# Moving two ScalarE operations of a weight conversion to its first step, and a subtraction behind the readers of a closed accumulator

## The chip, the cores and the metric

The kernel runs on one core of one Trainium2 chip. The metric is the device time of one execution in microseconds (us). The core's engines run side by side, each through its own list of instructions in order, and wait for each other by semaphores. PE is TensorE (matrix products, with PEld its weight loads), DVE is VectorE, ACT is ScalarE, POOL is GpSimd, SP only issues transfers.

## What is computed

An attention block with a position bias feeds a gated layer, and that feeds a second gated layer with a normalisation. Cut to what matters here:

```python
x = attention(q, k, v, bias)                  # 1152 tokens x 512
gate = 1.0 / (1.0 + np.exp(-(x @ w_gate)))    # 512 x 1536
val = x @ w_val
x = (gate * val) @ w_out                      # 1536 x 512
xn = x / rms(x) * rms_g                       # second layer
g = xn @ w_gate2
out = (g * sigmoid(g) * (xn @ w_val2)) @ w_out2
```

All matrix products of the two gated layers are made from split operands: a value is a high part that the fast product form holds exactly, and a low part that is the rest. Each product is three matmuls: high by high, high by low, low by high.

## The kernel before

**Weights.** They arrive as 64-bit numbers and are converted on the chip. One piece is 128 x 512 weights, loaded as pairs of 32-bit words (`wr`: the low word `lw`, the high word `hw`, so each word stands 8 bytes from the next of its kind). There are 72 pieces. `piece_step(k, i)` is one of four steps ("micro steps") on piece k. Step 0: DVE shifts the high word (`tt`, L471). Step 1: ACT takes the absolute value (`ab`, L480), DVE joins the sign (`ff`, L482), ACT scales the low word (`rb`, L484), and POOL adds it (`ff`, L485). Step 2: DVE multiplies (`ab`, L489), and ACT writes the high part into a ring of 24 slots (`wh` or `wv`, L490). Step 3: DVE subtracts to get the low part (`wl` or `wv`, L494).

**Order of the micro steps.** `advance(limit, micro)` issues micro steps: it goes round the four kinds in a fixed order and issues one whose `ready` is true. `tt` and `rb` have one buffer each, `ff` two, `ab` and `wr` three. `fetch` issues a load when the piece two before has passed step 1.

**The gated layers.** `STEPS` lists 72 steps s: a layer, a group g of 2 to 4 blocks of 128 hidden rows, a chunk c of 384 tokens, and a block f of the group. `gate_val(s)` issues 24 matmuls on PE (`gv`, L509), then `sg` on ACT (L513), `g` on DVE (L515), `gh` on ACT (L517). `low_part(s)` is one DVE subtraction (`gl`, L523). `out_mm(s)` is 12 matmuls (L539) into an accumulator `acc` of four PSUM parts, two pairs of banks. On PE the order is gv(s), out(s-2), gv(s+1), out(s-1) and so on. When a group's blocks for a chunk are all in, the accumulator is closed, and `collect` adds its four parts to `part` in SBUF: by four DVE additions (L547), and in the first group by two ACT copies (L551) and two DVE copies (L549). The next chunk's accumulator takes the same banks, so the next `out_mm` on PE waits for these readers. `closing(s - 2)` is true in the loop's step s in which the collect is issued. Some micro steps, five in most steps, are issued around `low_part` and `out_mm`; in a closing step all five follow.

**Before the gated layers** come 40 units of attention, the last eighteen with one micro step each, and a passage of four in which attention ends: there gv(0) is issued, and ACT evicts transposed blocks (`pt`, L703) that PE's product `pv` (L399) waits for.

Of the kernel before, what the change touches and what calls it, by code (L numbers as in the profile page):

```python
# [8 lines left out]
F32 = mybir.dt.float32  # L9
F32R = mybir.dt.float32r  # L10
U32 = mybir.dt.uint32
I32 = mybir.dt.int32
AF = mybir.ActivationFunctionType
ALU = mybir.AluOpType
# [60 lines left out]
def fused_kernel(ctx: ExitStack, tc: tile.TileContext, qk, vp, tab, pcol, invp, prm, wts, rg, out):  # L75
    nc = tc.nc
# [351 lines left out]
    def members(l, g):  # L428
        a = sum(GROUPS[l][:g])
        return range(a, a + GROUPS[l][g])  # L430
# [7 lines left out]
    NS = len(STEPS)  # L438
# [5 lines left out]
    wraw = {}  # L444
    mid = {}
# [21 lines left out]
    def piece_step(k, i):  # L467
        mc = pools["mc"]
        if i == 0:
            tt = mc.tile([128, 512], U32, tag="tt", name=f"tt{k}")  # L470
            nc.vector.tensor_scalar(  # L471
                tt, wraw[k][:, :, 1], 3, 0x3FFFFFFF, op0=ALU.logical_shift_left, op1=ALU.bitwise_and
            )
            mid[k] = tt
        elif i == 1:
            raw = wraw.pop(k)
            lw, hw = raw[:, :, 0], raw[:, :, 1]
            tt = mid[k]
            ab = mc.tile([128, 512], F32, tag="ab", name=f"ab{k}", bufs=3)
            nc.scalar.activation(ab, hw.bitcast(F32), AF.Abs)  # L480
            ff = mc.tile([128, 512], U32, tag="ff", name=f"ff{k}", bufs=2)
            nc.vector.scalar_tensor_tensor(ff, hw, 0xC0000000, tt, op0=ALU.bitwise_and, op1=ALU.bitwise_or)  # L482
            rb = mc.tile([128, 512], I32, tag="rb", name=f"rb{k}")
            nc.scalar.activation(rb, lw, AF.Copy, scale=2.0**-29)  # L484
            nc.gpsimd.tensor_tensor(ff.bitcast(I32), ff.bitcast(I32), rb, op=ALU.add)  # L485
            mid[k] = (ab, ff)
        elif i == 2:
            ab, ff = mid[k]
            nc.vector.scalar_tensor_tensor(ab, ab, TINY_HI, ff.bitcast(F32), op0=ALU.is_ge, op1=ALU.mult)  # L489
            nc.scalar.activation(ring[k % RING][0], ab, AF.Copy)  # L490
        else:
            ab, _ = mid.pop(k)
            hi, lo = ring[k % RING]
            nc.vector.tensor_tensor(lo, ab, hi.bitcast(F32), op=ALU.subtract)  # L494
            wp[PIECES[k]] = (hi, lo)
# [24 lines left out]
    def low_part(s):  # L520
        gh, g32 = gt[s]
        gl = pools["me"].tile([128, CH], F32R, tag="gl", name=f"gl{s}", bufs=3)
        nc.vector.tensor_tensor(gl, g32, gh.bitcast(F32), op=ALU.subtract)  # L523
        gt[s] = (gh, gl)

    def out_mm(s):
        l, g, c, f = STEPS[s]
        gh, gl = gt.pop(s)
        oh, ol = wp[l, f, 2]
        head, last = f == members(l, g)[0], f == members(l, g)[-1]  # L530
        final = g == len(GROUPS[l]) - 1
        if head:
            acc[c] = (bank2(f"acc{l}{g}{c}a"), bank2(f"acc{l}{g}{c}b"))
        a = acc[c]
        cs = slice(c * CH, c * CH + CH)
        def product(m):
            dst = a[m % 2][:, m // 2, :CH]
            for k, (st_, mv) in enumerate(((oh, gh), (oh, gl), (ol, gh))):
                nc.tensor.matmul(  # L539
                    dst, st_[:, m * 128 : m * 128 + 128], mv, start=(head and k == 0), stop=(last and k == 2)  # L540
                )

        def collect(m):
            dst = a[m % 2][:, m // 2, :CH]
            pt = part[m][:, cs]
            if g > 0:
                nc.vector.tensor_tensor(pt, dst, pt, op=ALU.add)  # L547
            elif m % 2:
                nc.vector.tensor_copy(pt, dst)  # L549
            else:  # L550
                nc.scalar.activation(pt, dst, AF.Copy)  # L551
            if final and l == 1:
                (nc.sync if m % 2 == 0 else nc.scalar).dma_start(out[m * 128 : m * 128 + 128, cs], pt)


        for m in range(NCC):
            product(m)
            if s == NS - 1:
                collect(m)
        if not last:  # L560
            return
        if s < NS - 1:
            for m in range(NCC):
                collect(m)
        if final and l == 0:
            norm_queue.append([s + 2, c, 0, None])
# [52 lines left out]
    done = [0, 0, 0, 0]  # L619
    loaded = [0]  # L620
    phase = [0]
# [7 lines left out]
    def closing(s):  # L629
        return 0 <= s < NS - 1 and STEPS[s][:3] != STEPS[s + 1][:3]  # L630
# [9 lines left out]
    def ready(i):  # L640
        k = done[i]
        if k >= (NPC if i == 0 else done[i - 1]):
            return False
        if i == 0:
            return k < loaded[0] and done[1] >= k
        if i == 1:
            return done[2] >= k - 1 and done[3] >= k - 2
        return i == 3 or k < room[0]
# [10 lines left out]
    def advance(limit, micro):  # L659
        room[0] = limit  # L660
        idle = 0
        while micro and idle < 4:
            fetch()
            i = (2, 1, 0, 3)[phase[0]]
            phase[0] = (phase[0] + 1) % 4
            if ready(i):
                piece_step(done[i], i)
                done[i] += 1
                micro -= 1
                idle = 0  # L670
            else:
                idle += 1
# [79 lines left out]
    for s in range(EARLY + MORE, RING):  # L752
        tag, size = ("pt", 9 * 128) if s < EARLY + MORE + 2 else ("v", 1024)
# [5 lines left out]
    for s in range(NS + 2):  # L759
        while s < NS and (STEPS[s][0], STEPS[s][3], 1) not in wp:  # L760
            advance(done[3] + 1, 1)
        if 0 < s < NS:
            gate_val(s)
        micro = pace(s)
        if any(q[0] <= s for q in norm_queue):
            micro = min(micro, 2)

        parts = (0, micro) if closing(s - 2) else (micro // 2, micro - micro // 2)
        for half in range(2):
            k = done[3]  # L770
            if k < NPC:
                lim = k
                while lim < NPC and lim < k + 3 and (lim < RING or released(lim - RING) <= s):
                    lim += 1
                advance(lim, parts[half])
            if half == 0:
                if s < NS:
                    low_part(s)
                if s > 1:
                    l, _, _, f = STEPS[s - 2]  # L780
                    while (l, f, 2) not in wp:
                        advance(done[3] + 1, 1)
                    out_mm(s - 2)
                while norm_queue and norm_queue[0][0] <= s:
                    _, c, stage, box = norm_queue.pop(0)
                    norm_stage(c, stage, box)
                    if stage < 3:
                        norm_queue.append([s + 1, c, stage + 1, box])
# [68 lines left out]
```

## Time and profile before

| what | value |
|---|---|
| time of the kernel before, median of 3 runs | 667.5 us (665.89 to 667.67) |
| the profiled execution's own time | 664.12 us |
| its span | 662.3 us |
| PE busy | 643.4 us, 97% |
| DVE, ACT, POOL busy | 454.8, 348.6, 211.6 us |
| granted TensorE clock | 0.999 of full speed |

The span runs from the first to the last instruction; the 1.8 us between it and the execution's time lie around it. Attention takes the first 198 us, and the two gated layers fill the rest. Busy shares tell little here: what counts is where PE stands still.

### The profile page before, as it was taken

The numbers are of one execution on the slowest core, as the hardware profiler recorded it, in microseconds if no ns is written. First come the engines' busy times: TensorE is split into PE (matmuls) and PEld (weight loads), VectorE is DVE, ScalarE is ACT, GpSimd is POOL, SyncE is SP. The second block draws the span as 40 slices with busy tenths as digits, with TensorE's granted clock in tenths as the row PEclk, the third lists the DMA queues.
The fourth block names the chain that finished last, engine by engine and source line by source line (L and its number), as shares of the span: only waits on it lengthen the run. The fifth ranks groups of instructions, "written<-read, shape, count | busy, mean of one in ns | idle before, by whom it ended". The sixth has DMA issues, their size and how long they took to land.

```text
span 662.3 us, 11825 instructions
## 1 busy us (share of the span) xinstructions
PE 643.4 (97%) x4454; PEld 575.6 (87%) x4454; DVE 454.8 (69%) x968; ACT 348.6 (53%) x743; POOL 211.6 (32%) x259
## 2 busy tenths in 40 slices
PE   8889999999999899999999999999999999999997
PEld 4236666777679899999999999999999999999997
DVE  6997898688656667867677678788777777321322
ACT  4648889798685555444444564553555545211110
POOL 6566677476453322222222221110223223000000
PEclk9999999999999999999999999999999999999999
DMA  8866855663124333323233332111234330000111
GB/s 212 276 234 191 226 185 184 232 215 98 50 66 127 104 120 95 96 97 102 93 112 108 96 95 65 64 55 42 84 108 117 98 105 33 1 0 1 48 48 48
DMA packets 28088, 71.73 MB, mean 108 GB/s; under 512 B 3456, under 2 KB 6528, under 8 KB 28032
## 3 DMA queue, kind: packets, MB, share of 16 engines
q1 hardware_dynamic: 27168, 69.80, 34.2%
q10 hardware_dynamic: 864, 1.18, 0.5%
q8 instruction: 35, 0.57, 0.3%
q14 instruction: 21, 0.17, 0.1%
HBM read 57.72 MB, written 13.25 MB: 107 GB/s over the span
## 4 chain that ended last, share of the span: by engine, by line
PE 61%; DVE 13%; ACT 12%; issue 5%; POOL 5%; POOLq 0%; DVEq 0%
PE gv L509 26%; PE s L310 6%; PE pv L399 6%; PE tp L379 6%; POOL ff L485 4%; DVE ab L489 4%; ACT ab L480 3%; ACT rb L484 3%; PE bps L211 3%; DVE part L547 2%; DVE g L515 2%; ACT sg L513 2%; ACT gh L517 1%; ACT wh L490 1%; DVE tt L471 1%
## 5 line engine op out<-in xcount | busy, mean ns | idle before, releaser
L485 POOL TENSOR_TENSOR ff<-ff,rb 128x512 int32<-128x512 int32 x72 | 96.5, 1341 | 284.5 <-ACT rb L484 216.2
L515 DVE TENSOR_TENSOR g<-gv,sg 128x384 f32<-128x384 f32 x72 | 40.1, 558 | 112.5 <-PE gv L509 66.7
L517 ACT ACTIVATE gh<-g 128x384 fp32r<-128x384 f32 x72 | 37.9, 526 | 76.4 <-DVE g L515 76.4
L509 PE MATMUL gv<-nh,wv 128*128 128x384 f32 x288 | 76.5, 337 | 0.0
L509 PE MATMUL gv<-xh,wh 128*128 128x384 f32 x216 | 73.2, 339 | 0.0
L509 PE MATMUL gv<-xl,wh 128*128 128x384 f32 x216 | 72.9, 337 | 0.0
L509 PE MATMUL gv<-xh,wl 128*128 128x384 f32 x216 | 72.9, 337 | 0.0
L489 DVE SCALAR_TENSOR_TENSOR ab<-ab,ff 128x512 f32<-128x512 f32 x72 | 49.9, 693 | 28.7 <-POOL ff L485 28.7
L361 POOL TENSOR_SCALAR p<-p,rs 128x576 f32<-128x576 f32 x72 | 60.4, 847 | 13.4 <-DVE rs L359 13.1
L490 ACT ACTIVATE wh<-ab 128x512 fp32r<-128x512 f32 x42 | 26.5, 631 | 66.9 <-DVE ab L489 66.8
L328 DVE CUSTOM_DVE_ANT_0 t<-s,bt 128x576 f32<-128x576 f32 x72 | 51.8, 751 | 13.8 <-PE s L310 12.3
L193 DVE TENSOR_SCALAR ht<-w1l,bpc 128x304 f32<-128x304 f32 (+17 forms) x100 | 58.8, 652 | 0.0
L513 ACT ACTIVATE sg<-gv 128x384 f32<-128x384 f32 x72 | 34.5, 479 | 44.9 <-PE gv L509 44.8
L349 ACT ACTIVATE p<-t,mn 128x576 f32<-128x576 f32 x72 | 55.2, 767 | 3.4 <-DVE mn L328 3.3
L310 PE MATMUL s<-raw 64*128 64x288 f32 (+1 forms) x320 | 52.6, 427 | 4.6 <-issue 3.1
L399 PEld LDWEIGHTS pv<-pt,v 128*64 128x64 f32 (+1 forms) x800 | 40.2, 136 | 16.8 <-ACT pt L703 10.2
L523 DVE TENSOR_TENSOR gl<-g,gh 128x384 fp32r<-128x384 f32 x72 | 40.1, 557 | 18.6 <-ACT gh L517 18.6
L509 PEld LDWEIGHTS gv<-nh,wv 128*128 128x128 f32 x288 | 52.4, 188 | 0.0
L399 PE MATMUL pv<-pt,v 128*64 128x128 f32 (+2 forms) x800 | 49.6, 268 | 1.0 <-ACT pt L703 1.0
L490 ACT ACTIVATE wv<-ab 128x512 fp32r<-128x512 f32 x30 | 19.0, 633 | 57.5 <-DVE ab L489 57.4
L482 DVE SCALAR_TENSOR_TENSOR ff<-wr,tt 128x512 uint32<-128x512 uint32 x72 | 49.2, 683 | 0.0
L509 PE MATMUL gv<-nh,wh 128*128 128x384 f32 x144 | 48.7, 338 | 0.0
(356 smaller groups left out, 1588.6 us busy)
## 6 DMA issues: line engine op xcount, KB each, us to landing
wr<-wts SPq DMA_DIRECT2D x72, 512.0 KB, 3.6
bias_d<-be SPq DMA_DIRECT2D x36, 295.5 KB, 3.8
bt<-bias_d SPq DMA_DIRECT2D x16, 576.0 KB, 4.8
raw<-qk SPq DMA_DIRECT2D x16, 288.0 KB, 6.3
v<-vp SPq DMA_DIRECT2D x8, 320.0 KB, 3.6
v<-vp SPq DMA_DIRECT2D x8, 160.0 KB, 4.8
bt<-bias_d SPq DMA_DIRECT2D x8, 144.0 KB, 3.2
out<-part SPq DMA_DIRECT2D x6, 192.0 KB, 1.8
```

What stands on the lines that cost most here:

```text
L193: nc.vector.tensor_scalar(ht, src, bpc[:, t : t + 1], 0.0, op0=ALU.add, op1=ALU.max)
L310: nc.tensor.matmul(dst, raw[r, 0, it * 128 : it * 128 + rows_of(it)], raw[r, 1, hf * 288 : hf * 288 + 288], start=True, stop=True,)
L328: nc.vector.tensor_tensor_reduce(t, sp[:, :, :288], bt[:, j].rearrange("p (a c) -> p a c", a=2), -SCALE, 3.0e38, ALU.add, ALU.min, mn[:, j ...
L349: nc.scalar.activation(p[:, j], t.rearrange("p a c -> p (a c)"), AF.Exp, bias=mn[:, j : j + 1], scale=-1.0, accum_out=sm[:, j : j + 1],)
L361: nc.gpsimd.tensor_scalar(p[:, j], p[:, j], rs[:, j : j + 1], 1.0, op0=ALU.mult, op1=ALU.mult)
L399: nc.tensor.matmul(box["ps"][j * 64 : j * 64 + 64, :n], v[:k, 2 * j if it == 4 else j, c, :], pt[:k, c, j * 64 : j * 64 + 64] if it == 4 e ...
L482: nc.vector.scalar_tensor_tensor(ff, hw, 0xC0000000, tt, op0=ALU.bitwise_and, op1=ALU.bitwise_or)
L485: nc.gpsimd.tensor_tensor(ff.bitcast(I32), ff.bitcast(I32), rb, op=ALU.add)
L489: nc.vector.scalar_tensor_tensor(ab, ab, TINY_HI, ff.bitcast(F32), op0=ALU.is_ge, op1=ALU.mult)
L490: nc.scalar.activation(ring[k % RING][0], ab, AF.Copy)
L509: nc.tensor.matmul(ps[:, :CH], wt[:, cs], xt[:, cc, :], start=(k == 0), stop=(k == 11))
L515: nc.vector.tensor_tensor(g32, pss[1][:, :CH], sg, op=ALU.mult)
```

## The change

Three edits. The absolute value and the low word's scaling move from step 1 to step 0 of a piece; the scaled low word is written over the raw low word instead of into `rb`, the shifted word stands in `ff` (now three buffers) instead of `tt`. The rules of readiness and the round of the four kinds change with it. And in a closing step `low_part(s)` is issued behind `out_mm(s - 2)` and its collects instead of ahead of them.

```diff
--- before.py
+++ after.py
@@ -467,23 +467,20 @@
     def piece_step(k, i):
         mc = pools["mc"]
         if i == 0:
-            tt = mc.tile([128, 512], U32, tag="tt", name=f"tt{k}")
-            nc.vector.tensor_scalar(
-                tt, wraw[k][:, :, 1], 3, 0x3FFFFFFF, op0=ALU.logical_shift_left, op1=ALU.bitwise_and
-            )
-            mid[k] = tt
+            raw = wraw[k]
+            lw, hw = raw[:, :, 0], raw[:, :, 1]
+            ff = mc.tile([128, 512], U32, tag="ff", name=f"ff{k}", bufs=3)
+            nc.vector.tensor_scalar(ff, hw, 3, 0x3FFFFFFF, op0=ALU.logical_shift_left, op1=ALU.bitwise_and)
+            ab = mc.tile([128, 512], F32, tag="ab", name=f"ab{k}", bufs=3)
+            nc.scalar.activation(ab, hw.bitcast(F32), AF.Abs)
+            nc.scalar.activation(lw.bitcast(I32), lw, AF.Copy, scale=2.0**-29)
+            mid[k] = (ab, ff)
         elif i == 1:
             raw = wraw.pop(k)
             lw, hw = raw[:, :, 0], raw[:, :, 1]
-            tt = mid[k]
-            ab = mc.tile([128, 512], F32, tag="ab", name=f"ab{k}", bufs=3)
-            nc.scalar.activation(ab, hw.bitcast(F32), AF.Abs)
-            ff = mc.tile([128, 512], U32, tag="ff", name=f"ff{k}", bufs=2)
-            nc.vector.scalar_tensor_tensor(ff, hw, 0xC0000000, tt, op0=ALU.bitwise_and, op1=ALU.bitwise_or)
-            rb = mc.tile([128, 512], I32, tag="rb", name=f"rb{k}")
-            nc.scalar.activation(rb, lw, AF.Copy, scale=2.0**-29)
-            nc.gpsimd.tensor_tensor(ff.bitcast(I32), ff.bitcast(I32), rb, op=ALU.add)
-            mid[k] = (ab, ff)
+            ab, ff = mid[k]
+            nc.vector.scalar_tensor_tensor(ff, hw, 0xC0000000, ff, op0=ALU.bitwise_and, op1=ALU.bitwise_or)
+            nc.gpsimd.tensor_tensor(ff.bitcast(I32), ff.bitcast(I32), lw.bitcast(I32), op=ALU.add)
         elif i == 2:
             ab, ff = mid[k]
             nc.vector.scalar_tensor_tensor(ab, ab, TINY_HI, ff.bitcast(F32), op0=ALU.is_ge, op1=ALU.mult)
@@ -642,7 +639,7 @@
         if k >= (NPC if i == 0 else done[i - 1]):
             return False
         if i == 0:
-            return k < loaded[0] and done[1] >= k
+            return k < loaded[0] and done[1] >= k - 1 and done[2] >= k - 2 and done[3] >= k - 2
         if i == 1:
             return done[2] >= k - 1 and done[3] >= k - 2
         return i == 3 or k < room[0]
@@ -661,7 +658,7 @@
         idle = 0
         while micro and idle < 4:
             fetch()
-            i = (2, 1, 0, 3)[phase[0]]
+            i = (0, 2, 1, 3)[phase[0]]
             phase[0] = (phase[0] + 1) % 4
             if ready(i):
                 piece_step(done[i], i)
@@ -774,13 +771,15 @@
                     lim += 1
                 advance(lim, parts[half])
             if half == 0:
-                if s < NS:
+                if s < NS and not closing(s - 2):
                     low_part(s)
                 if s > 1:
                     l, _, _, f = STEPS[s - 2]
                     while (l, f, 2) not in wp:
                         advance(done[3] + 1, 1)
                     out_mm(s - 2)
+                if closing(s - 2):
+                    low_part(s)
                 while norm_queue and norm_queue[0][0] <= s:
                     _, c, stage, box = norm_queue.pop(0)
                     norm_stage(c, stage, box)
```

The number of instructions on each engine stays the same, and so does the number of micro steps in each of the 72 steps. Below, names end in the buffer's number; `g_18` is step 18's.

DVE, from step 18 (an ordinary step) to the start of step 19 (a closing one), before:

```order
L515 TENSOR_TENSOR g_18_4198<-gv_1_4183,sg_4196 128x384
L482 SCALAR_TENSOR_TENSOR ff_4204<-wr_4037,tt_4165 128x512
L471 TENSOR_SCALAR tt_4211<-wr_4101 128x512
L523 TENSOR_TENSOR gl_4213<-g_18_4198,gh_4200 128x384
L494 TENSOR_TENSOR wl_1793<-ab_4140,wh_1792 128x512
L489 SCALAR_TENSOR_TENSOR ab_4202<-ab_4202,ff_4204 128x512
L482 SCALAR_TENSOR_TENSOR ff_4232<-wr_4101,tt_4211 128x512
L515 TENSOR_TENSOR g_19_4265<-gv_1_4250,sg_4263 128x384
L523 TENSOR_TENSOR gl_4269<-g_19_4265,gh_4267 128x384
L547 TENSOR_TENSOR part_3045<-acc020a,part_3045 128x384
L547 TENSOR_TENSOR part_3046<-acc020b,part_3046 128x384
L547 TENSOR_TENSOR part_3047<-acc020a,part_3047 128x384
```
and in the changed kernel:

```order
L512 TENSOR_TENSOR g_18_4141<-gv_1_4126,sg_4139 128x384
L482 SCALAR_TENSOR_TENSOR ff_4106<-wr_3981,ff_4106 128x512
L491 TENSOR_TENSOR wl_1793<-ab_4048,wh_1792 128x512
L520 TENSOR_TENSOR gl_4150<-g_18_4141,gh_4143 128x384
L473 TENSOR_SCALAR ff_4164<-wr_4043 128x512
L486 SCALAR_TENSOR_TENSOR ab_4108<-ab_4108,ff_4106 128x512
L482 SCALAR_TENSOR_TENSOR ff_4164<-wr_4043,ff_4164 128x512
L512 TENSOR_TENSOR g_19_4201<-gv_1_4186,sg_4199 128x384
L544 TENSOR_TENSOR part_3028<-acc020a,part_3028 128x384
L544 TENSOR_TENSOR part_3029<-acc020b,part_3029 128x384
L544 TENSOR_TENSOR part_3030<-acc020a,part_3030 128x384
L544 TENSOR_TENSOR part_3031<-acc020b,part_3031 128x384
```
In step 18 the low part `wl` of the older piece has moved up to directly behind `ff`, and the next piece's shift (now L473, into `ff`) behind `gl`. In step 19 the four additions from `acc020` stand ahead of `gl`.

ACT, from step 18's `sg` to step 19's, before:

```order
L513 ACTIVATE sg_4196<-gv_0_4170 128x384
L517 ACTIVATE gh_4200<-g_18_4198 128x384
L480 ACTIVATE ab_4202<-wr_4037 128x512
L484 ACTIVATE rb_4206<-wr_4037 128x512
L490 ACTIVATE wh_1794<-ab_4202 128x512
L480 ACTIVATE ab_4230<-wr_4101 128x512
L484 ACTIVATE rb_4234<-wr_4101 128x512
L513 ACTIVATE sg_4263<-gv_0_4237 128x384
```
and in the changed kernel (L475 is the absolute value, L476 the low word in place, L487 the high part):

```order
L510 ACTIVATE sg_4139<-gv_0_4113 128x384
L514 ACTIVATE gh_4143<-g_18_4141 128x384
L475 ACTIVATE ab_4166<-wr_4043 128x512
L476 ACTIVATE wr_4043<-wr_4043 128x512
L487 ACTIVATE wh_1794<-ab_4108 128x512
L510 ACTIVATE sg_4199<-gv_0_4173 128x384
```
Before, the absolute value and `rb` of a piece stand directly ahead of its own `wh`, and behind the `wh` of the piece before. Now those two rows belong to the piece after: `wh_1794` is made from `ab_4108`, which was issued in the step before.

ACT at the end of attention, from step 0's `gh`, before:

```order
L517 ACTIVATE gh_2934<-g_0_2932 128x384
L703 ACTIVATE pt_2936<-tp_0_2937 128x512
L703 ACTIVATE pt_2936<-tp_4_2942 64x128
L411 ACTIVATE xf_2962<-pv_2951 128x64
L417 ACTIVATE xh_119<-xf_2962 128x64
L490 ACTIVATE wh_1792<-ab_2897 128x512
L703 ACTIVATE pt_2968<-tp_0_2969 128x512
L480 ACTIVATE ab_2977<-wr_2640 128x512
L484 ACTIVATE rb_2981<-wr_2640 128x512
L703 ACTIVATE pt_2968<-tp_4_2974 64x128
```
and in the changed kernel:

```order
L514 ACTIVATE gh_2922<-g_0_2920 128x384
L700 ACTIVATE pt_2924<-tp_0_2925 128x512
L475 ACTIVATE ab_2938<-wr_2632 128x512
L476 ACTIVATE wr_2632<-wr_2632 128x512
L700 ACTIVATE pt_2924<-tp_4_2930 64x128
L411 ACTIVATE xf_2953<-pv_2942 128x64
L417 ACTIVATE xh_119<-xf_2953 128x64
L487 ACTIVATE wh_1792<-ab_2869 128x512
L700 ACTIVATE pt_2959<-tp_0_2960 128x512
L700 ACTIVATE pt_2959<-tp_4_2965 64x128
```
Two conversions now stand between the two evictions (`pt`) of the first of these two units; before, two stood between those of the second.

## Rows read from the trace of the kernel before

**Rows 1.** Page, part 1: busy us, share of the span, instructions.
```profile
PE 643.4 (97%) x4454; PEld 575.6 (87%) x4454; DVE 454.8 (69%) x968; ACT 348.6 (53%) x743; POOL 211.6 (32%) x259
```
**Rows 2.** Windows: us, then busy time (instructions) of PE, PEld, DVE, ACT, POOL, clock, DMA.
```profile
200.00:400.00 200.00, 194.54 (x1107) 192.43 (x1106) 143.92 (x255) 101.28 (x191) 52.89 (x40) 1.00 0.34 105
400.00:600.00 200.00, 200.00 (x1157) 200.00 (x1156) 135.88 (x267) 88.91 (x168) 34.72 (x26) 1.00 0.19 61
```
**Rows 3.** Waits of PE's weight loads, 200 to 400 us: us, times, longest.
```profile
PEld acc001a L539 <- ACT part L551: 2.3, 1, 2.3
PEld acc021a L539 <- issue: 1.6, 1, 1.6
PEld acc020a L539 <- issue: 1.6, 1, 1.6
PEld ss L587 <- issue: 1.1, 1, 1.1
```
**Rows 4.** Chain that ended last, 470 to 500 us: start, us, what.
```profile
484.57 4.17 PE gv L509 x24
...
490.85 4.17 PE gv L509 x24
```
**Rows 5.** Timeline of ACT: sg of steps 9 and 21. Start, us, operation.
```profile
255.74 0.48 ACT L513 ACTIVATE sg<-gv 128x384 f32<-128x384 f32 x1
...
334.07 0.47 ACT L513 ACTIVATE sg<-gv 128x384 f32<-128x384 f32 x1
```
**Rows 6.** Timeline of DVE, step 18 and the start of closing step 19.
```profile
316.19 0.56 DVE L515 TENSOR_TENSOR g<-gv,sg 128x384 f32<-128x384 f32 x1 [1.08 <-ACT sg L513]
316.66 0.68 DVE L482 SCALAR_TENSOR_TENSOR ff<-wr,tt 128x512 uint32<-128x512 uint32 x1
317.38 0.43 DVE L471 TENSOR_SCALAR tt<-wr 128x512 uint32<-128x512 uint32 x1
317.72 0.55 DVE L523 TENSOR_TENSOR gl<-g,gh 128x384 fp32r<-128x384 f32 x1
318.19 0.69 DVE L494 TENSOR_TENSOR wl<-ab,wh 128x512 fp32r<-128x512 f32 x1
320.05 0.69 DVE L489 SCALAR_TENSOR_TENSOR ab<-ab,ff 128x512 f32<-128x512 f32 x1 [1.18 <-POOL ff L485]
320.66 0.69 DVE L482 SCALAR_TENSOR_TENSOR ff<-wr,tt 128x512 uint32<-128x512 uint32 x1
322.93 0.56 DVE L515 TENSOR_TENSOR g<-gv,sg 128x384 f32<-128x384 f32 x1 [1.58 <-ACT sg L513]
324.07 0.56 DVE L523 TENSOR_TENSOR gl<-g,gh 128x384 fp32r<-128x384 f32 x1 [0.59 <-ACT gh L517]
324.55 0.55 DVE L547 TENSOR_TENSOR part<-acc020a,part 128x384 f32<-128x384 f32 x1
...
325.94 0.55 DVE L547 TENSOR_TENSOR part<-acc020b,part 128x384 f32<-128x384 f32 x1
```
**Rows 7.** Timeline of ACT in step 18.
```profile
317.21 0.67 ACT L480 ACTIVATE ab<-wr 128x512 f32<-128x512 f32 x1
317.77 0.67 ACT L484 ACTIVATE rb<-wr 128x512 int32<-128x512 uint32 x1
320.78 0.63 ACT L490 ACTIVATE wh<-ab 128x512 fp32r<-128x512 f32 x1 [2.33 <-DVE ab L489]
...
322.42 0.47 ACT L513 ACTIVATE sg<-gv 128x384 f32<-128x384 f32 x1
```
**Rows 8.** Timeline of POOL in step 18.
```profile
318.52 1.50 POOL L485 TENSOR_TENSOR ff<-ff,rb 128x512 int32<-128x512 int32 x1 [4.14 <-ACT rb L484]
322.59 1.30 POOL L485 TENSOR_TENSOR ff<-ff,rb 128x512 int32<-128x512 int32 x1 [2.57 <-ACT rb L484]
```
**Rows 9.** Timelines of POOL and DVE at 267 us.
```profile
267.31 1.46 POOL L485 TENSOR_TENSOR ff<-ff,rb 128x512 int32<-128x512 int32 x1 [6.12 <-DVE ff L482]
267.55 1.78 DVE L494 TENSOR_TENSOR wv<-ab,wv 128x512 fp32r<-128x512 f32 x1
```
**Rows 10.** Timeline of PE at the end of attention.
```profile
198.17 0.33 PE L399 MATMUL pv<-pt,v 64*64 64x64 f32 x4 [0.59 <-ACT pt L703]
```

## The prediction

> **What bounds the kernel now.** I read the page first: PE is busy for 97% of the span [rows 1], so all that can be won is the time in which PE stands still. The windows say where: from 400 to 600 us PE and its weight loads are busy throughout, from 200 to 400 us they lack 5 to 8 us [rows 2]. The waits of the weight loads name the places: 2.3 us at the head of acc001, 1.6 us each at acc020 and acc021, 1.1 us at the norm's product ss, 6.6 us in all [rows 3]; three waits of 0.3 us I leave out. At each of the first three PE wants the banks of an accumulator whose readers are late. The page's releaser "issue" there means only that the last one to release it is not named on that row.
>
> Why late? PE needs 490.85 - 484.57 = 6.28 us for a step without waits [rows 4]. The other engines need more. From sg of step 9 to sg of step 21 are 334.07 - 255.74 = 78.3 us [rows 5]; PE alone would need 12 x 6.28 = 75.4. The difference, 2.9, is nearly the two waits of 1.6 us in that stretch. So between 200 and 400 us the vector side (DVE, ACT and POOL together) sets the pace, and PE pays what it is over.
>
> Step 18 shows what the vector side does in its 6.74 us (g at 316.19, next g at 322.93) [rows 6]. DVE stands idle for 1.18 us until POOL's sum is there, then for 1.58 us until sg is there. Behind both is one chain: ACT's absolute value at 317.21 and rb at 317.77, which ends at 318.44; then POOL at 318.52; DVE's ab at 320.05; ACT's wh at 320.78, and only behind wh and the next pair of conversions sg, at 322.42 [rows 6 to 8]. ACT is in order, and the conversions of a piece stand behind the wh of the piece before: each piece goes through ACT, ACT, POOL, DVE, ACT one after the other.
>
> **The change part by part.** No instruction is added or removed. *Moved conversions.* ACT's two conversions of a piece now stand ahead of the wh of the piece before, and need only the load. POOL's sum waits then for DVE's ff alone, and sg no longer stands behind wh plus two conversions in step 18.
>
> I walk through step 18 in its new order, g, ff, wl, gl, shift, ab, ff. On DVE the next instruction starts 0.47 us after g or gl, about 0.60 after a piece's operation, 0.34 after the shift [rows 6]. From g at 0: ff at 0.47, wl at 1.07, gl at 1.67 (gh is there: g to gl took 324.07 - 322.93 = 1.14 where DVE waited for gh [rows 6]), shift at 2.14 to 2.57. POOL could begin its sum at 1.2, when ff is done. But DVE's wl and POOL's sum do not run side by side: at 267.55 a wl that began during a sum took 1.78 us instead of 0.69 and ended 0.56 behind the sum [rows 6, 9], and at 318.52 a sum that began during a wl took 1.50 instead of 1.30 [rows 8]. In the old order the sums mostly met an idle DVE; in the new one wl follows ff directly, so nearly every sum collides. I take the worst order, also for gl and the shift: the sum runs from 2.57 to 3.87. Then ab at 3.90, wh at 4.62, sg at 5.16, g at 5.66. Instead of 6.74, so 1.1 us less.
>
> The rule behind the collision is in the Trainium skill, SBUF — State Buffer, Who interferes with whom: VectorE with two SBUF inputs and GpSimd take one port pair as an exclusive lock. It speaks against this change, and the trace agrees with it, by the 1.78 us. Without such a lock step 18 would take some 4.3 us, by it 5.7.
>
> For the average I lay everything that excludes each other end to end. A piece: shift 0.34, ff 0.60, ab 0.61, low part 0.60, sum 1.30, handovers 0.05, in all 3.5 us; five micro steps are 1.25 pieces, so 15 pieces in the twelve steps, 52.5 us. Twelve g and gl at 0.94: 11.3. Four closings with four additions at (325.94 - 324.55)/3 = 0.46: 7.4 [rows 6]. Sum 71.2. The twelve steps walked one by one as above give 72.5, since low parts wait for wh here and there. Either is under PE's 75.4. The vector side then drops from 0.24 us over PE to about 0.24 under it, in each step, and the waits at acc020, acc021 and ss lose their cause: 1.6 + 1.6 + 1.1 = 4.3 us.
>
> *Two prices that no row shows.* ACT now writes every second word, and POOL reads every second word. ACT's conversions already read every second word, and at 0.67 take hardly longer than wh at 0.63, which reads them side by side [rows 7]; DVE's shift reads so as well, in 0.43 [rows 6]. So I take nothing for both. The upper bound for ACT is another 0.67, which hides, as ACT is far from full. That for POOL is a third stream beside its two, so half more: 1.30 to 1.95. This one does not hide, see the first rival.
>
> *gl behind the collects.* In closing step 19 the additions start 324.55 - 322.93 = 1.62 us after g, since gl waits for gh first [rows 6]; now 0.47 after. So the banks are free 1.15 us sooner. gl itself comes some 1.4 us later, but is wanted by out_mm two steps on; cover is a whole step of PE, 6.28. With the vector side ahead this edit adds nothing; with it behind, it shifts each reader once by 1.15.
>
> *First wait.* At acc001 PE waits for ACT copies (L551) [rows 3], which stand behind gh as before, so only the speed counts. Up to there lie the passage, which I leave equal (its micro steps run along a chain of 4 us a piece before, along the collisions now), and steps 1 and 2. Step 2 has the order of step 18, so saves 1.1; step 1 by the same walk saves 0.5. Of 2.3 us stay 0.7.
>
> *End of attention.* Two conversions, 2 x 0.67 less overlap 0.1, now lie ahead of the second eviction of one unit. There PE already waited 0.59 for an eviction [rows 10], and the later unit loses two conversions in return. Between 0 and 1.2 us; I take 0.3. In the units before, the same ACT work lies in another unit of the same length, so nothing.
>
> *Loads.* A raw piece is free when POOL has read it, no longer when ACT has: up to 1.3 us later, with about two pieces of lead. Nothing; if loads were late, ACT would stop at the conversions and sg with it.
>
> Sum: 4.3 + (2.3 - 0.7) - 0.3 = 5.6 us less. The profiled execution took 664.12 us, so 658.5. The median of the runs is 667.5, 3.4 above it; the same saving gives **661.9 us**.
>
> **The rivals.** *Slower: POOL's strided read costs.* Place: the sum, L485. At 1.95 us twelve steps need 72.5 + 15 x 0.65 = 82.3, which is 0.57 a step over PE. From step 3 to 29 that is 15 us, from 41 to 56 another 8.5, less the 4.3 us by which PE's next head lets readers be late: about 19 in place of 6.6, so 680 us. It bites from 0.2 us more a sum (75.4 - 72.5 over 15) and decides at 0.4 (78.3 - 72.5 over 15). For it speaks that no sum here reads so; against it that neither DVE nor ACT pay for such reads.
>
> The Trainium skill, GPSIMD Engine Reference, section 7, has a rule near it: reads by steps of more than 8 bytes cost half more. Here the step is 8 bytes exactly, so by the rule nothing; no row of before shows it.
>
> *Collisions take it all back.* If POOL and DVE block each other more than I laid end to end (a low part that waits for wh, lets the sum in, and so starts the next piece late), the vector side stays at its 78.3. PE's waits are then what the vector side is over, and only the collects' shift is left, once: 667.5 - 1.2 = 666.3. For it speaks that the pair is taken for some 4.8 of 6.0 us in a step; against it that the walk already holds it.
>
> *Half of it.* The passage at the end of attention goes badly by 1.2 and the first wait stays at 2.3: 4.3 - 1.2 = 3.1 less, 664.4 us.
>
> **How the numbers follow.** Forecast 0.65, half of it 0.12, taken back 0.13, slower 0.10. A measurement of this kernel tells about 0.3%, 2 us, from no change. So faster 0.77, same 0.13, slower 0.10. The forecast's own range is 659.6 (all 6.6 saved, and a microsecond between runs) to 663.5. The range for 8 in 10 reaches up over half of it and most of the taken-back case: 659.6 to 667.4. The slower rival stays outside.
>
> **What the profile of the changed kernel would show.** Right: POOL's sum released by DVE's ff (L482), no more by ACT; sums of 1.3 us alone and up to 2.5 where wl and gl run; g of step 18 to that of 19 under 6 us; no waits of PE at acc020, acc021 and ss, and under 1 us at acc001; from sg to sg 6.28 a step, PE's pace, with DVE waiting for PE. Wrong: a sum that takes over 1.5 us with no DVE beside it; waits of PE at accumulator heads past 250 us; evictions that hold PE between 190 and 199 us for more than 2 us; ACT idle for a load.

## The result and the profile after

The changed kernel takes 658.76 us (median of 4 runs, 656.57 to 659.28), the kernel before, beside it on the same chip, 666.69 us. The ratio is 0.9888, 95% interval 0.9865 to 0.9911: faster by 7.9 us, where a saving of 5.6 and a time of 661.9 us were forecast. The profiled span fell from 662.3 to 654.8 us, by 7.5.

The page's first part after the change, and its row for POOL's sum (busy us, mean ns, then idle time and what ended it):

```profile
PE 641.7 (98%) x4454; PEld 575.8 (88%) x4454; DVE 486.7 (74%) x968; ACT 349.0 (53%) x743; POOL 227.4 (35%) x259
...
L483 POOL TENSOR_TENSOR ff<-ff,wr 128x512 int32<-128x512 int32 x72 | 113.2, 1573 | 250.9 <-DVE ff L482 130.8
```

DVE and POOL are busier with the same number of instructions, by 32 and 16 us [rows 1]: more of their work now falls at the same time, and they block each other. On DVE 27.5 of the 32 us lie in one group, the shift. Its rows before and after (count, busy us, mean ns):

```profile
L471 DVE TENSOR_SCALAR tt<-wr 128x512 uint32<-128x512 uint32 x72 | 34.7, 481 | 1.5
...
L473 DVE TENSOR_SCALAR ff<-wr 128x512 uint32<-128x512 uint32 x72 | 62.1, 863 | 0.0
```

In the changed kernel 34 of the 72 shifts run beside no POOL work and take 0.42 us, and 34 overlap a sum and take 1.34 us on average. Each of these 34 ends 0.28 or 0.29 us after the sum. So the sum holds up this operation of one input too, not only those of two. PE lost its idle time, and the windows show where, as in [rows 2]:

```profile
200.00:400.00 200.00, 200.00 (x1150) 199.83 (x1149) 172.71 (x274) 102.56 (x195) 65.13 (x41) 1.00 0.35 105
400.00:600.00 200.00, 200.00 (x1156) 200.00 (x1155) 138.69 (x248) 87.93 (x166) 39.53 (x26) 1.00 0.20 61
```

Of the waits of [rows 3] one of 0.2 us is left, at acc001; acc020, acc021 and ss have none:

```profile
PEld acc001a L536 <- ACT part L548: 0.2, 1, 0.2
```

**Where the 7.5 us lie.** Three instructions on PE's timeline cut the span: the first product of the gated layers (of gv(0)), the head (first product) of acc010 and the head of acc122, the last accumulator. After:

```profile
188.28 0.44 PE L506 MATMUL gv<-xh,wh 128*128 128x384 f32 x1
...
244.48 0.34 PE L536 MATMUL acc010a<-gh,wh 128*128 128x384 f32 x1
...
638.33 0.34 PE L536 MATMUL acc122a<-gh,wv 128*128 128x384 f32 x1
```

Before:

```profile
189.06 0.44 PE L509 MATMUL gv<-xh,wh 128*128 128x384 f32 x1
...
247.46 0.44 PE L539 MATMUL acc010a<-gh,wh 128*128 128x384 f32 x1
...
645.88 0.34 PE L539 MATMUL acc122a<-gh,wv 128*128 128x384 f32 x1
```

From the start to gv(0), which stands among the last units of attention: 0.78 us less. From there to acc010, the stretch A: 58.40 before, 56.20 after, 2.20 less. From acc010 to acc122, the stretch B: 398.42 before, 393.85 after, 4.57 less. Together 7.55. These two stretches measure all kernels below, since they leave out the clock's changes in attention (last section). They also leave out what a kernel wins or loses in the units just ahead of gv(0), which matters for e4 and e10.

**Step 18 after the change**, and the start of closing step 19, on DVE (start, us, operation, idle time ahead and its releaser), to be laid beside [rows 6]:

```profile
308.70 0.56 DVE L512 TENSOR_TENSOR g<-gv,sg 128x384 f32<-128x384 f32 x1 [1.08 <-ACT sg L510]
309.17 0.68 DVE L482 SCALAR_TENSOR_TENSOR ff<-wr,ff 128x512 uint32<-128x512 uint32 x1
309.77 0.69 DVE L491 TENSOR_TENSOR wl<-ab,wh 128x512 fp32r<-128x512 f32 x1
310.37 1.68 DVE L520 TENSOR_TENSOR gl<-g,gh 128x384 fp32r<-128x384 f32 x1
311.97 0.42 DVE L473 TENSOR_SCALAR ff<-wr 128x512 uint32<-128x512 uint32 x1
312.31 0.68 DVE L486 SCALAR_TENSOR_TENSOR ab<-ab,ff 128x512 f32<-128x512 f32 x1
312.91 0.68 DVE L482 SCALAR_TENSOR_TENSOR ff<-wr,ff 128x512 uint32<-128x512 uint32 x1
314.07 0.56 DVE L512 TENSOR_TENSOR g<-gv,sg 128x384 f32<-128x384 f32 x1 [0.48 <-ACT sg L510]
315.39 0.56 DVE L544 TENSOR_TENSOR part<-acc020a,part 128x384 f32<-128x384 f32 x1 [0.77 <-PE acc020a L536]
...
317.31 0.55 DVE L520 TENSOR_TENSOR gl<-g,gh 128x384 fp32r<-128x384 f32 x1
```

ACT in the same step, where [rows 7] stood:

```profile
309.72 0.66 ACT L475 ACTIVATE ab<-wr 128x512 f32<-128x512 f32 x1
310.28 0.67 ACT L476 ACTIVATE wr<-wr 128x512 int32<-128x512 uint32 x1
313.02 0.63 ACT L487 ACTIVATE wh<-ab 128x512 fp32r<-128x512 f32 x1 [2.07 <-DVE ab L486]
313.56 0.47 ACT L510 ACTIVATE sg<-gv 128x384 f32<-128x384 f32 x1
```

And POOL, where [rows 8] stood:

```profile
309.99 1.64 POOL L483 TENSOR_TENSOR ff<-ff,wr 128x512 int32<-128x512 int32 x1 [3.86 <-DVE ff L482]
313.72 1.31 POOL L483 TENSOR_TENSOR ff<-ff,wr 128x512 int32<-128x512 int32 x1 [2.10 <-ACT wh L487]
```

From g to g are now 314.07 - 308.70 = 5.37 us, 6.74 before. sg follows wh directly, and POOL's sum is released by DVE's ff: both sums start 0.13 us after their ff ends, also the one at 313.72, where the profile names ACT's wh, which ended last. The first sum starts during wl and takes 1.64 us, and the gl behind it waits: 1.68 us in place of 0.55. In closing step 19 the collects wait 0.77 us for PE, which is still at work on their accumulator: they are no longer late, they are early. That holds for every accumulator from acc010 to acc032: the last reader ends 1.86 us after PE's last product starts, where before it took 2.1 to 6.1.

### The profile page after: what moved, and what is told of

It is laid out like the page before. It is cut to its first block, busy times and chain, and to the rows that moved or that the text cites. A ratio compares the mean times of both kernels' runs of the same rounds, so it can differ in the third digit from the quotient of the medians.

```text
span 654.8 us, 11812 instructions
## 1 busy us (share of the span) xinstructions
PE 641.7 (98%) x4454; PEld 575.8 (88%) x4454; DVE 486.7 (74%) x968; ACT 349.0 (53%) x743; POOL 227.4 (35%) x259
## 4 chain that ended last, share of the span: by engine, by line
PE 92%; DVE 1%; issue 1%; ACT 1%; POOL 1%; POOLq 0%; DVEq 0%
PE gv L506 46%; PE pv L399 7%; PE s L310 7%; PE tp L379 6%; PE bps L211 3%; PE acc122a L536 1%; PE acc102b L536 1%; PE acc100b L536 1%; PE acc121b L536 1%; PE acc101b L536 1%; PE acc120b L536 1%; PE acc030b L536 1%; PE acc032b L536 1%; PE acc112b L536 1%; PE acc111b L536 1%
## 5 line engine op out<-in xcount | busy, mean ns | idle before, releaser
L483 POOL TENSOR_TENSOR ff<-ff,wr 128x512 int32<-128x512 int32 x72 | 113.2, 1573 | 250.9 <-DVE ff L482 130.8
L361 POOL TENSOR_SCALAR p<-p,rs 128x576 f32<-128x576 f32 x72 | 59.0, 830 | 14.1 <-DVE rs L359 13.7
L473 DVE TENSOR_SCALAR ff<-wr 128x512 uint32<-128x512 uint32 x72 | 62.1, 863 | 0.0
L487 ACT ACTIVATE wh<-ab 128x512 fp32r<-128x512 f32 x42 | 26.4, 630 | 45.2 <-DVE ab L486 44.7
L520 DVE TENSOR_TENSOR gl<-g,gh 128x384 fp32r<-128x384 f32 x72 | 45.3, 629 | 7.0 <-ACT gh L514 7.0
L482 DVE SCALAR_TENSOR_TENSOR ff<-wr,ff 128x512 uint32<-128x512 uint32 x72 | 49.1, 683 | 0.0
```

The costliest lines, as they stand in the source:

```text
L361: nc.gpsimd.tensor_scalar(p[:, j], p[:, j], rs[:, j : j + 1], 1.0, op0=ALU.mult, op1=ALU.mult)
L473: nc.vector.tensor_scalar(ff, hw, 3, 0x3FFFFFFF, op0=ALU.logical_shift_left, op1=ALU.bitwise_and)
L482: nc.vector.scalar_tensor_tensor(ff, hw, 0xC0000000, ff, op0=ALU.bitwise_and, op1=ALU.bitwise_or)
L483: nc.gpsimd.tensor_tensor(ff.bitcast(I32), ff.bitcast(I32), lw.bitcast(I32), op=ALU.add)
```

## The experiments

The theory at the start is called the **chain**: PE waited because ACT made a piece's two operations behind the wh of the piece before, and their move is what pays; gl's move adds next to nothing. Its rivals: that the edit of gl, the extra buffers, or the new round of the micro steps carry the gain. What was measured, all in one table (A and B in us, from each kernel's trace as above; "ss" is the norm's product of [rows 3]):

| kernel | ratio to before (95%) | A | B | waits over 0.3 us at heads and ss, in A; in B |
|---|---|---|---|---|
| before | 1 | 58.40 | 398.42 | 2.3; 1.6, 1.6, 1.1 |
| after | 0.9888 (0.9865 to 0.9911) | 56.20 | 393.85 | none; none |
| e1 moves only | 0.9894 (0.9868 to 0.9919) | 56.53 | 393.85 | none; none |
| e2 low rows only | 0.9943 (0.9921 to 0.9966) | 59.44 | 393.85 | 2.5; none |
| e3 buffers only | 0.9967 (0.9950 to 0.9984) | 59.38 | 396.10 | 2.2; 1.5, 0.8 |
| e4 ACT's order only | 0.9914 (0.9887 to 0.9941) | 56.58 | 393.69 | none; none |
| e5 half a pass more | 0.9909 (0.9892 to 0.9926) | 57.26 | 393.84 | 1.3; none |
| e6 a pass more | 0.9932 (0.9911 to 0.9954) | 58.16 | 394.01 | 0.7; none |
| e7 second eviction earlier | 0.9885 (0.9868 to 0.9901) | 56.21 | 393.85 | none; none |
| e8 one more shift buffer | 0.9980 (0.9963 to 0.9996) | 58.03 | 397.44 | 2.1; 1.2, 1.5, 0.9 |
| e9 the gap filled | 0.9936 (0.9912 to 0.9960) | 58.20 | 393.85 | 2.5; none |
| e10 ACT's order and low rows | 0.9913 (0.9892 to 0.9934) | 56.75 | 393.68 | none; none |

In e2 and e3 A is longer than before, although the waits are not: the clock fell there behind the wait at acc001 (last section). B can hardly come below 393.7: from acc010 to acc122 PE then has no wait at a head left to lose.

**e1, the conversions without gl's edit.** The changed kernel, with `low_part` at its old place:

```diff
-                if s < NS and not closing(s - 2):
+                if s < NS:
                     low_part(s)
...
-                if closing(s - 2):
-                    low_part(s)
```

> The changed kernel, but the low gated rows are subtracted ahead of the collects as before; only the conversions are moved. Chain theory (ACT's conversions stood behind the high part of the piece before, and so set the pace of the vector side): nearly the whole gain stays, about 7 of 8 us, ratio to before 0.988 to 0.991, no wait of PE at accumulator heads past 250 us. Rival (the earlier readers of a closed accumulator bring the gain): at least half is lost, ratio above 0.994, waits at acc020 and acc021 return.

Measured 660.19 us, B as after, A 0.33 us more. The moved conversions, with the new round, rules and buffers, bring nearly all, as the chain says.

**e2, gl's edit alone**, the same lines put into the kernel before.

> The kernel before, with only the low gated rows moved behind the collects of a closed accumulator. Chain theory: the vector side keeps its 78 us for twelve steps, so PE's waits are only put off once: 0.5 to 1.5 us less, ratio 0.998 to 0.999, waits at accumulator heads stay above 3 us in sum. Rival (the earlier readers bring the gain): 3 us or more, ratio below 0.9955.

Measured 661.51 us. Here the chain theory fails: B is 393.85 us, the same as after, and the only wait left between 200 and 440 us is that of 2.5 us at acc001. The trace says why. DVE in closing step 19:

```profile
322.25 0.56 DVE L515 TENSOR_TENSOR g<-gv,sg 128x384 f32<-128x384 f32 x1 [1.58 <-ACT sg L513]
322.72 0.55 DVE L547 TENSOR_TENSOR part<-acc020a,part 128x384 f32<-128x384 f32 x1
...
324.58 0.55 DVE L523 TENSOR_TENSOR gl<-g,gh 128x384 fp32r<-128x384 f32 x1
```

In [rows 6] DVE stood idle for 0.59 us between g and gl, since gh was not yet there. Now the additions run in that gap, and gl finds gh done. That is not a shift once, but time won in each closing step: from g to g, steps 10, 16, 19 and 22 take 8.44, 6.30, 6.60 and 8.43 us in place of 9.11, 6.98, 7.30 and 9.14, and only step 13 takes 0.16 more. By sg, steps 9 to 21 take 76.4 us in place of 78.3 [rows 5].

That is still 1.0 us over PE's 75.4, and yet PE waits at no head there. The traces show how late readers may be: before, the last readers of acc012 and acc020 end 6.1 us after PE's last product on each starts, and PE waits 1.6 us each time; in e3 they end 4.7 and 6.0 us after it, and PE waits 0.2 and 1.5. So PE waits for what goes beyond some 4.5 us. In e2 they end after 3.3 and 4.2 us, within this margin.

**e9, the same gap filled otherwise.** The kernel before, with one micro step ahead of gl in a closing step; the additions still stand behind gl:

```diff
-        parts = (0, micro) if closing(s - 2) else (micro // 2, micro - micro // 2)
+        parts = (1, micro - 1) if closing(s - 2) else (micro // 2, micro - micro // 2)
```

> The kernel before, but in a closing step one of the five micro steps is issued ahead of the low part and the collects instead of behind them; gl stays ahead of the collects. Filling theory (moving gl paid because DVE's 0.6 us of idle time behind g in each closing step was filled): here the gap is filled too, by a shift, a join or a product, while the collects still stand behind gl and start no sooner than before. So the waits at acc020, acc021 and ss go or shrink to under half, and the ratio is 0.993 to 0.997. Early-readers theory (it paid because the four additions from the accumulator came 1.15 us sooner): here they come no sooner, so those waits stay as they were, acc001 may gain another 0.5 to 1 us where an ACT conversion now stands ahead of its copies, and the ratio is 0.999 to 1.003.

Measured 661.68 us, B 393.85 again. DVE in closing step 19:

```profile
319.18 0.56 DVE L515 TENSOR_TENSOR g<-gv,sg 128x384 f32<-128x384 f32 x1 [1.58 <-ACT sg L513]
319.65 0.77 DVE L471 TENSOR_SCALAR tt<-wr 128x512 uint32<-128x512 uint32 x1
320.35 0.54 DVE L523 TENSOR_TENSOR gl<-g,gh 128x384 fp32r<-128x384 f32 x1
320.82 0.54 DVE L547 TENSOR_TENSOR part<-acc020a,part 128x384 f32<-128x384 f32 x1
```

The additions start 1.64 us after g, as late as before (1.62), and yet the waits in B are gone. So an earlier start of the additions within the step is not needed; filling the gap is enough. It is barely enough: the last readers of acc012 and acc020 end 3.5 and 4.4 us behind PE. That e2 won some 0.7 us in each such step, near the 0.59 that stood idle, fits filling as the cause there too, but e2's edit also starts the additions earlier, and no run separates the two. In some steps of e9 the piece ahead of gl gained more than 0.6 us (step 10 takes 7.30 in place of 9.11), so an earlier start of that piece's chain counts too; how the two share was not taken apart.

**e4, only ACT's order.** The kernel before, old round, old rules, old place of gl; ACT's two operations move to step 0, into buffers of their own (a second `rb`; one of the 24 ring slots moves to another pool to make room):

```diff
         if i == 0:
...
-            mid[k] = tt
+            lw, hw = wraw[k][:, :, 0], wraw[k][:, :, 1]
+            ab = mc.tile([128, 512], F32, tag="ab", name=f"ab{k}", bufs=3)
+            nc.scalar.activation(ab, hw.bitcast(F32), AF.Abs)
+            rb = mc.tile([128, 512], I32, tag="rb", name=f"rb{k}", bufs=2)
+            nc.scalar.activation(rb, lw, AF.Copy, scale=2.0**-29)
+            mid[k] = (tt, ab, rb)
```

> The kernel before with only ACT's two conversions of a piece moved to its first step, into buffers of their own (two for the scaled low word), with the old round of steps, the old rules, the old place of the low gated rows and nothing in place. DVE's and POOL's orders are those of before. Chain theory: ACT's order alone gives the gain between 200 and 400 us, some 6 to 7 us, ratio 0.989 to 0.992; the first product of the gated layers stays at 189 us, where the whole change had it at 188.3. Rival (the new round of steps or the writing in place matters): ratio above 0.995.

Measured 660.16 us. The waits of PE's weight loads between 200 and 440 us are this one row, an eviction's:

```profile
PEld pv L399 <- ACT pt L704: 0.7, 1, 0.7
```

ACT's order alone takes away every wait at a head; the result in place, the new round and the new rules carry none of that. The second `rb` is not what does it: with it and more buffers, but in the old order, e3 below keeps most of the waits. As expected, gv(0) wins nothing here, see e10.

**e10, e4 and gl's edit together**, so the change without its buffers in place, its round and its rules.

> The kernel before with ACT's two operations moved to the first step, into buffers of their own, in the old round and by the old rules, and with the low part behind the collects in closing steps: the changed kernel without the result in place, without the new round and rules and without the third buffer of ff. Theory that these two moves are the whole change: no waits at accumulator heads past 200 us, and a ratio of 0.986 to 0.992, the changed kernel's within a measurement. Rival (the new round and the third buffer carry a part of their own): 0.2 to 0.4% slower than the changed kernel, with lags at the collects above 1.9 us.

Measured 661.03 us, no waits at heads, and the readers 1.86 us behind from acc010 on, as after. By B the two moves are the whole change. By the ratio it is not decided: 0.9913 is 0.25% above after's 0.9888, which is what the rival named, and the intervals overlap. The traces go further. PE of e10 at the end of attention:

```profile
183.27 0.76 PE L379 MATMUL tp<-ident,p 128*128 128x128 f32 x5
...
191.78 0.95 PE L399 MATMUL pv<-pt,v 128*64 128x64 f32 x20 [0.78 <-ACT pt L704]
192.66 0.44 PE L510 MATMUL gv<-xh,wh 128*128 128x384 f32 x1
...
200.14 0.95 PE L399 MATMUL pv<-pt,v 128*64 128x64 f32 x20 [0.93 <-ACT pt L704]
201.54 0.69 PE L399 MATMUL pv<-pt,v 128*64 128x64 f32 x16 [0.45 <-ACT pt L704]
202.82 0.33 PE L399 MATMUL pv<-pt,v 64*64 64x64 f32 x4 [0.60 <-ACT pt L704]
```

The same transposes (`tp`, at 183.27) start at 179.84 us before and at 179.74 after. From them to gv(0) it is 9.22 us before, 8.54 after and 9.39 in e10; from gv(0) to gv(1) 9.37, 9.75 and 10.43. Of these four waits the changed kernel has only those of 0.93 and 0.45. The other two, 0.78 and 0.60, arise where ACT's two conversions stand ahead of an eviction that has none ahead of it in the changed kernel, in e4 as in e10. Where a conversion falls is a matter of the order of issue, so of the round and the rules; e3 and e8, which move ring slots too, have the waits of before there. These therefore carry a part: 0.85 us before gv(0) and 0.55 in A, less 0.17 in B, some 1.2 us against e10. In that the rival was right, not in the later readers that it expected.

**e3 and e8, buffers alone.** The kernel before, first with second buffers of `tt` and `rb` and a third of `ff`, then with the second `tt` alone. Two ring slots (in e8 one) move to another pool to make room, so e8 is not quite one buffer "and nothing else":

```diff
-            tt = mc.tile([128, 512], U32, tag="tt", name=f"tt{k}")
+            tt = mc.tile([128, 512], U32, tag="tt", name=f"tt{k}", bufs=2)
...
-            ff = mc.tile([128, 512], U32, tag="ff", name=f"ff{k}", bufs=2)
+            ff = mc.tile([128, 512], U32, tag="ff", name=f"ff{k}", bufs=3)
...
-            rb = mc.tile([128, 512], I32, tag="rb", name=f"rb{k}")
+            rb = mc.tile([128, 512], I32, tag="rb", name=f"rb{k}", bufs=2)
```

> The kernel before in its old order, with two buffers for the shifted word, three for the joined word and two for the scaled low word; two ring slots lie in the other pool to make room, and the order on every engine is the same. Chain theory: the waits that these buffers take away are never the last, so within 0.5 us of before, ratio 0.999 to 1.001. Rival (a lack of buffers, above all the single one of the scaled low word that waits for POOL, sets the pace): 4 us or more less, ratio below 0.994.

> The kernel before with two buffers for the shifted word instead of one, nothing else. If the 0.12 us by which the shift starts later behind the joined word, because it writes over its input, is what the three buffers together took away, 15 x 0.12 = 1.8 us in twelve steps go, and this kernel gives the same as all three: 1.5 to 3 us less, ratio 0.9955 to 0.998. Rival (the scaled low word's single buffer counts, on which ACT waits for POOL): within 0.7 us of before, ratio above 0.999.

Measured 664.34 and 664.41 us, by the ratios 2.2 and 1.3 us faster than before, and in B by 2.3 and 1.0. With all three buffers the waits of PE's weight loads are, without an eviction's and a short one:

```profile
PEld acc001a L539 <- ACT part L551: 2.2, 1, 2.2
PEld acc021a L539 <- issue: 1.5, 1, 1.5
...
PEld ss L587 <- issue: 0.8, 1, 0.8
...
PEld acc020a L539 <- issue: 0.2, 1, 0.2
```

The wait at acc020 shrinks from 1.6 to 0.2, the other large ones stay. e3 lies between its theories, e8 at the near edge of the one on the shift: step 18 takes 6.61 us there and 6.62 in e3, in place of 6.74, the 0.12 that was expected, but twelve steps gain 0.5 us by sg, not 1.8. Buffers help a little, and they are no substitute for ACT's order, which removes all of these waits.

**e5 and e6, POOL made slower.** The changed kernel, with one more pass of POOL over each piece behind the sum, a multiplication by one, over half of the columns (`w` 256) or all (512):

```diff
+            f = ff.bitcast(F32)[:, :w]
+            nc.gpsimd.tensor_scalar(f, f, 1.0, 1.0, op0=ALU.mult, op1=ALU.mult)
```

> The changed kernel with one more POOL operation per piece, behind its sum and on half of its columns (times one, in place, some 0.4 us). Pace theory (the vector side needs at most 72.5 us for twelve steps, less by the third of a microsecond a step that step 18 measured under my walk, against PE's 75.4): 15 x 0.4 = 6 us more puts it at PE's pace, so within 2 us of the changed kernel, ratio to before 0.988 to 0.992, with the lag of the gated rows behind PE grown. Rival (the vector side is far from PE's pace since the change): nothing at all moves, no larger lag.

> The same with the POOL operation on all columns (some 0.75 us a piece). Pace theory: 15 x 0.75 = 11 us more in twelve steps puts the vector side 5 to 8 us over PE's 75.4, so PE waits at accumulator heads again, 10 to 20 us in all over the steps with conversions, ratio to before 1.00 to 1.02. Rival (room is left): ratio 0.988 to 0.992.

Measured 660.75 and 662.03 us. The groups of POOL's instructions in e6 (count, busy us, mean ns) show that the pass is there:

```profile
L483 POOL TENSOR_TENSOR ff<-ff,wr 128x512 int32<-128x512 int32 x72 | 113.2, 1572 | 199.1 <-ACT wh L489 52.8 <-ACT wv L489 45.2 <-issue 34.7
...
L485 POOL TENSOR_SCALAR ff<-ff 128x512 f32<-128x512 f32 x72 | 54.4, 756 | 6.3
```

It adds 1.25 x 0.756 = 0.94 us of POOL's time to each step, four times the 0.24 that I gave the vector side to spare, and B grows by 0.16 us. The 10 to 20 us of waits that the pace theory expected did not come, and in e5 the readers in B are no later than after (1.86 us). So there was more room than that, or the pass lies beside work of DVE; these runs don't tell which. What e6 lost against after lies in A: 0.7 us at acc001, and a slower clock from 200 to 206 us (below).

**e7, the wait that is left.** The changed kernel, with the second eviction (`E1`) ahead of the micro steps (`C`) in the order of the last four units:

```diff
-    "M0 T X0 E2 N Q E0 M1 C X1 E1 B L P0 P1 V",
+    "M0 T X0 E2 N Q E0 E1 M1 C X1 B L P0 P1 V",
```

> The changed kernel; at the end of attention the second eviction of a unit is issued ahead of that unit's conversions instead of behind them. If the two conversions ahead of the eviction are what PE's product waits 0.9 us for at 195 us, that wait goes and all that follows comes 0.5 to 1 us sooner: ratio to before 0.986 to 0.989. Rival (the wait only moves to the next unit's eviction, or the weights come later): within 0.3 us of the changed kernel.

Measured 658.69 us, no difference from after. The wait moved to the next eviction, as the rival said: 1.47 us in one piece where after has 0.93 and 0.45. PE there:

```profile
198.93 0.95 PE L399 MATMUL pv<-pt,v 128*64 128x64 f32 x20 [1.47 <-ACT pt L700]
```

No version beats the changed kernel by more than a measurement tells.

## Why the prediction was right in direction and too small

**Right.** What bounds the kernel (PE, and its waits where readers were late); that ACT's order held the vector side back (e4 moves little else and removes every wait at a head); the 4.3 us at acc020, acc021 and ss, which all went (B: 4.57); POOL released by DVE's ff; the steps from sg to sg at PE's pace (75.6 us for steps 9 to 21).

**The step that failed: the cap on the gain.** I put 6.6 us as all that could be won, from waits between 200 and 400 us alone [rows 3], and let the end of attention only cost. Three terms of the sum were wrong, and all in one direction. Of the 3.1 us between the 661.9 forecast and the 658.76 measured, 2.3 are this saving; 0.8 are the level, since the forecast started from a median of 667.5 and the kernel before took 666.69 beside the changed one. (The lower end of the range, 659.6, is by its own words 667.5 - 6.6 - 1 = 659.9.)

*End of attention, forecast 0.3 lost, measured 0.4 won.* The evictions did cost what I took, 0.38: PE waits 0.93 and 0.45, where it waited 0.41 and 0.59 before (the second is [rows 10]):

```profile
195.75 0.95 PE L399 MATMUL pv<-pt,v 128*64 128x64 f32 x20 [0.93 <-ACT pt L700]
197.15 0.95 PE L399 MATMUL pv<-pt,v 128*64 128x64 f32 x20 [0.45 <-ACT pt L700]
```

But for the units before I wrote that the same ACT work lies in another unit of the same length, "so nothing", and did not look at what waited for it. Before, POOL stood 1.57 us for rb there, its sum came late, the normalisation `p` behind it came late, and PE waited:

```profile
185.19 1.52 POOL L485 TENSOR_TENSOR ff<-ff,rb 128x512 int32<-128x512 int32 x1 [1.57 <-ACT rb L484]
...
187.49 0.77 PE L379 MATMUL tp<-ident,p 128*128 128x128 f32 x5 [0.62 <-POOL p L361]
```

After, the sum runs without a wait, 1.7 us earlier:

```profile
183.49 1.28 POOL L483 TENSOR_TENSOR ff<-ff,wr 128x512 int32<-128x512 int32 x1
```

PE's wait at `tp` is gone, and gv(0) starts 0.78 us earlier; 0.1 of that was there already at 180 us (179.84 against 179.74). It is the same mechanism as in the gated layers, at a place where I had only counted ACT's time. But ACT's order wins here only together with the new round: in e4 and e10 `tp` does not wait either, and an eviction behind the conversions takes 0.78 us instead.

*First wait, forecast 0.7 left, measured 0.2.* From gv(1) (198.43 before, 198.03 after) to the head of acc001 (221.81, 219.26) are 2.15 us less, where I took 1.6: the walk gave too little. *Three waits of 0.3 us*, which I left out, went too: from acc001 to acc010 it is 0.43 less, and B is 0.27 beyond my 4.3. So 0.70 + 0.55 + 0.43 + 0.27 = 1.95 of the span lie outside the sum, and the medians differ by 0.4 more than the spans: that is the distance from 5.6 to 7.9.

**Step 18: 5.66 forecast, 5.37 measured.** The walk put the sum behind wl, gl and the shift as the worst order. The sum went directly behind wl, and gl waited instead. The Trainium skill, SBUF — State Buffer, Who interferes with whom, says that issue order decides who blocks; by that the sum, begun at 309.99, goes ahead of gl at 310.37, and the trace agrees, with the 1.68 us of gl. I had used the rule's lock and not its order.

**gl's edit: the reason was wrong.** "With the vector side ahead this edit adds nothing" holds beside the conversions (e1 against after). "With it behind, it shifts each reader once by 1.15" does not: alone it brings 4.57 us in B, by some 0.7 us in most closing steps (e2). Twelve steps were 2.9 us over PE, and four closing steps give back 1.9 of that, enough to stay within the 4.5 us that readers may be late; either edit alone carries B. Only A needs ACT's order: there the readers are ACT's copies, behind gh.

**The slower rival** fell by one row: a sum beside which DVE ran only g, which took its usual 0.56, takes 1.31 us (313.72) where [rows 8] had 1.30. The Trainium skill's rule in GPSIMD Engine Reference, section 7, that only steps of more than 8 bytes cost half more, is met by that row for a step of 8. ACT's write in place costs nothing either: 0.67 us at 310.28. **Collisions take it all back**: the sums rose to a mean of 1.573 us from 1.341, and the shifts, which the sum of 3.5 us a piece has at 0.34, to 0.863 from 0.481, but they did not set the pace (B; e6).

## What to carry to other kernels

An in-order engine that prepares inputs for two others should do so before it takes up the results of the piece before; look for every consumer that waits for it, in each phase of the program, not only in the one where the bottleneck waits. A stall of half a microsecond at a place that comes once in three steps is a rate, not an offset: fill it with any work that is ready. When two edits both remove the same shortfall, test each alone, as together they hide one another. And when an order of issue changes, look at each phase that it runs through: here the same move won or lost half a microsecond and more at the end of attention, by where the conversions fell.

## What the runs showed of the hardware

PE's granted clock fell in places that the change doesn't touch. In the windows from 30 to 50 us it was 1.00 in the profiles of before, after and e9, and 0.59 to 0.83 in the others. In e1, whose attention has the order of after, gv(0) came 3.6 us later (191.84 against 188.28); that is why A and B are counted from gv(0) on. e1 in that window:

```profile
30.00:50.00 20.00, 17.14 (x105) 8.09 (x104) 14.96 (x39) 7.68 (x17) 8.20 (x12) 0.66 0.66 223
```

It also was low behind some waits of PE. In e2, behind the wait at acc001 (220 to 224 us), and in e6, behind the evictions at 197 to 199:

```profile
220.00:224.00 4.00, 1.86 (x9) 1.53 (x8) 3.19 (x7) 2.06 (x5) 1.26 (x1) 0.88 0.49 131
224.00:230.00 6.00, 6.00 (x30) 6.00 (x29) 4.78 (x9) 4.02 (x8) 1.29 (x1) 0.80 0.31 87
```

```profile
200.00:206.00 6.00, 6.00 (x28) 6.00 (x27) 5.39 (x8) 2.98 (x7) 3.62 (x5) 0.72 0.49 124
```

PE did 30 matmuls from 224 to 230 us where before did 36 at 1.00, and 28 in e6 where the next six microseconds have 36. So a part of these 6 us ran at 1.2 GHz in place of 2.4, and PE lost one to one and a half microseconds beyond the wait. e3 is alike behind its wait at acc001: 0.75 from 226 to 232 us, with 27 matmuls. Behind the same waits the clock was 1.00 in before, e8 and e9 (acc001) and in after (the evictions); what decides it stays open.
